# Attention ahead of two MLPs on one core: K transposed like Q, small products in row tiles, bounds by TensorE, and a new order of steps

## The chip, the core and the metric

The kernel runs on one core of a Trainium2 chip. The metric is the device time of one launch in microseconds (us), taken as the median of three runs. A profile of one further execution goes with it. TensorE's matrix products are called PE here, its weight loads PEld, VectorE DVE, ScalarE ACT, GpSimd POOL, and the queue that issues the DMAs SP.

## The reference, cut to what matters

Three parts follow one another. Attention works on two batches of eight heads, 576 positions of 64 numbers, everything in float32:

```python
# factor 4: q, k, v are averaged over groups of 4 positions -> 144 positions
out_d = softmax(q_d @ k_d.T / 8) @ v_d            # whole attention over 144
out_up = repeat(out_d, 4)
mask = abs(pos_q - pos_k) < 4                     # local attention, 7 keys wide
out_local = softmax(where(mask, q @ k.T / 8, -1e9)) @ v
x = out_up + out_local                            # 1152 tokens x 512
```

Then a soft mixture of eight experts, `out += P[:, e] * (relu(x @ w1[e]) @ w2[e])` with `P` from eight rounds of row and column normalisation of a gate, and an MLP with a Mish activation and widths 512, 2048, 512.

## The kernel before, in words

Big products run in float16: each operand is split into a high and a low float16 part after it was scaled by a power of two, and three products replace one. The scale comes from a bound of the operand, so the kernel needs a bound of V (for x), of W1[0], of W2[0], of W1[1] and of the gate before it can split them.

Work is laid out by pairs of heads: pair j of batch b holds two heads in 128 partitions. Pairs 0 to 3 are batch 0, pairs 4 to 7 batch 1. One string, `ORDER`, lists the steps of the eight pairs and of the first expert; the program emits them in that order, and each engine takes its instructions strictly as they were emitted. A step may name its engine (`:V` DVE, `:A` ACT, `:G` POOL). The steps, with the pair's number behind the name:

- LQ, LK, LV, LW load q, k, v by groups of four (tile `vm`) and v by windows of 32 keys (tile `vw`).
- TP transposes 288 columns of q or k by PE (line 654); TQ (659) copies q's to `qt`, TK (558 or 556) k's to `kt`. `kt` holds the two heads of a pair in separate column blocks with zeros in the other head's partitions, so that one product over 128 partitions gives both heads. K is loaded in runs of six positions, so TK writes with a stride and in quarters. SQ and SK (677 on DVE, 681 and 682 on POOL) sum groups of four.
- Local scores: QL (690, 695) adds the mask and 24 products of 32 queries by 64 columns. LM, SU, EL, LS, LN (711 to 737) are the softmax, TR (744) transposes 32 by 32 blocks on DVE, BD (558, 556) copies four pieces of it to a block-diagonal tile `bd`, AV (811) multiplies by `vw`.
- Averaged attention: QD (704), DM (759), ED (770), DS (776), DN (783), AP (794) transposes, AE copies, AD (819) multiplies by `vd`, which VP (627, 628) sums from `vm`.
- UP (825), XF (831), XH (837), XL (840) join both, scale them, and write the two float16 parts of x.
- VQ (619) squares `vm`, WM (175) squares or takes the maximum of a quarter of a weight tensor, WT, WP, WR, WQ, WE turn the partial bounds into a scale; WH and WL (195, 226) write the two parts of W1[0] and W2[0].
- M and R (914, 923) are the products of the first expert's first layer for one block of 128 features and 288 tokens; here tokens of batch 0 only. H and I write its float16 parts, N and E (1069) are the second layer for 128 tokens.

M needs x of all four pairs of batch 0, because it sums over all heads, and both parts of W1[0]. From the first M on, the steps of batch 1 stand between M and N. After `ORDER` come the gate (1137), the products of batch 1, seven more experts and the last MLP; nothing in them is touched. PSUM has eight banks: two for M and N, six for attention (`at`), of which QD and AV take two each.

Of the kernel before, what the change touches and what calls it, by code (L numbers as in the profile page):

```python
# [10 lines left out]
F32 = mybir.dt.float32  # L11
# [10 lines left out]
def attn_moe_moe2_kernel(ctx: ExitStack, tc: tile.TileContext, q, k, v, w_gate, w1, w2, w_in, w_out, out):  # L22
# [124 lines left out]
    class Split:  # L147
# [35 lines left out]
        def bound(self):  # L183
            m1 = sm.tile([128, 1], F32, tag="m1", name="m1")
            nc.vector.tensor_reduce(out=m1, in_=self.mx, axis=AX.X, op=ALU.add if self.squares else ALU.max)
            return m1

# [312 lines left out]
    ones = const.tile([128, 128], F32, name="ones")  # L500
    ss = const.tile([128, B, NP], F32, name="ss")
# [10 lines left out]
    spare_at, spare_dve = acc[:, NTT - 5, 0:384], acc[:, NTT - 4, :]  # L512
    spare_pool = acc[:, NTT - 3:NTT - 1, :].rearrange("p t d -> p (t d)")
# [7 lines left out]
    def emit_consts(t, mask):  # L521
# [13 lines left out]
        nc.vector.tensor_copy(out=ident16, in_=ident)  # L535
        nc.vector.memset(ones, 1.0)
        nc.vector.memset(ss, 0.0)
# [4 lines left out]
        nc.vector.tensor_copy(out=mask.rearrange("p g h c -> p (g h) c"),  # L542
                              in_=edge.unsqueeze(1).to_broadcast([128, 2 * G, 32]))

        nc.vector.memset(mask[0:32, 0, :, 0:3], SHUT)
        nc.vector.memset(mask[96:128, G - 1, :, 27:32], SHUT)
# [5 lines left out]
    spare_up = []  # L552

    def copy_on(eng, out, in_):
        if eng == "A":
            nc.scalar.activation(out=out, in_=in_, func=AF.Copy)  # L556
        else:
            tensor_engine(eng).tensor_copy(out=out, in_=in_)

    xs = [None, None]  # L560

    class Attention:
        def __init__(self, b, pools, at_tile):
            self.b, self.p, self.at = b, pools, at_tile
            self.qm, self.km, self.vm, self.vw, self.st = {}, {}, {}, {}, {}

        def load_qk(self, src, j):

            t = self.p["qk"].tile([96, 12, D], F32, tag="qk", name="qk")
            for h in range(2):  # L570
                a = src[self.b, 2 * j + h]
                if src is q:
                    nc.sync.dma_start(out=t.rearrange("p (u h) d -> p u h d", h=2)[:, :, h],
                                      in_=a.rearrange("(u p) d -> p u d", p=96))
                else:
                    nc.sync.dma_start(out=t[:, 6 * h:6 * h + 6], in_=a.rearrange("(p u) d -> p u d", u=6))
            return t

        def load_vm(self, j):

            t = self.p["vm"].tile([HM, 2, 2, 4, D], F32, tag="vm", name="vm")
            nc.sync.dma_start(out=t.rearrange("p h a r d -> p (h a) (r d)"),
                              in_=v[self.b, 2 * j:2 * j + 2].rearrange("h (a p r) d -> p (h a) (r d)", a=2, r=4))
            self.vm[j] = t
# [32 lines left out]
        def VQ(self, j):  # L617
            t = self.vm[j]
            nc.scalar.activation(out=spare_act[0:HM, :], in_=t.rearrange("p h a r d -> p (h a r d)"), func=AF.Square,
                                 accum_out=ss[0:HM, self.b, j:j + 1])  # L620

        def VP(self, j, eng):
            t = self.vm[j]
            vd = self.p["vd"].tile([HM, 2, 2, D], F32, tag="vd", name="vd")
            eng, room = (nc.vector, spare_dve) if eng == "V" else (nc.gpsimd, spare_pool)
            v2 = room[0:HM, 0:512].rearrange("p (h a r d) -> p h a r d", h=2, a=2, r=2)
            eng.tensor_tensor(out=v2, in0=t[:, :, :, 0:2, :], in1=t[:, :, :, 2:4, :], op=ALU.add)
            eng.tensor_tensor(out=vd, in0=v2[:, :, :, 0, :], in1=v2[:, :, :, 1, :], op=ALU.add)
            self.st["vd", j] = vd

        def bound(self):
            m1 = sm.tile([128, 1], F32, tag="mv", name="mv")
            nc.vector.tensor_reduce(out=m1, in_=ss[:, self.b, :], axis=AX.X, op=ALU.add)
            return m1

        def scale(self, ma):
# [3 lines left out]
            self.sxq = const.tile([128, 1], F32, name=f"sxq{b}")  # L640
            nc.vector.tensor_scalar(out=self.sxq, in0=self.sx, scalar1=0.25, scalar2=None, op0=ALU.mult)
# [7 lines left out]
        def TP(self, j, n, i):  # L649

            t = self.st["qk"[n], j]
            ps = self.at()[:, 0:288]
# [5 lines left out]
        def TQ(self, j, i):  # L658
            nc.scalar.activation(out=keep["qt"][j % 2][:, 288 * i:288 * i + 288], in_=self.st["T", j, 0, i],
                                 func=AF.Copy, scale=QSC)  # L660

        def TK(self, j, h, u, eng):

            to = keep["kt"][j % 2][64 * h:64 * h + 64, h, 3:3 + S].rearrange("c (p u r) -> c u p r", u=3, r=2)
            copy_on(eng, to[:, :, :, u],
                    self.st["T", j, 1, h][64 * u:64 * u + 64].rearrange("c (u p) -> c u p", u=3))

        def SQ(self, j, eng):
            self.pool_sum(keep["qd"][j % 2].unsqueeze(1), keep["qt"][j % 2][:, 0:S].unsqueeze(1), eng)

        def SK(self, j, eng):
            self.pool_sum(keep["kd"][j % 2], keep["kt"][j % 2][:, :, 3:3 + S], eng)

        def pool_sum(self, out, t, eng):
            t = t.rearrange("c h (m r) -> c h m r", r=4)
# [3 lines left out]
            n = out.shape[1]  # L679
# [1007 lines left out]
```

## Time and profile before

| | |
|---|---|
| three runs | 998.66, 994.86, 996.56 us; median 996.56 |
| profiled execution, its own time | 997.51 us |
| its span, first to last instruction | 995.7 us, so 1.8 us lie around it |
| busy | PE 964.9 us (97%), DVE 678.6 (68%), ACT 533.6 (54%), POOL 74.9 (8%) |
| HBM | 73.15 MB read, 14.94 MB written, 88 GB/s over the span |
| TensorE's clock, mean | 0.985 of 2.4 GHz |

A busy PE is one with a product under way; the ends of products are modelled. The clock is given as a share: 1.00 is 2.4 GHz, 0.50 is 1.2 GHz, and what lies between is a mean over a stretch that had both.

### The profile page before, as it was taken

Reading aid. Unit: us, or ns where it says so; the run is one execution under the profiler, and the core shown is the slowest. Engines: PE = TensorE matmul, PEld = TensorE weight load, DVE = VectorE, ACT = ScalarE, POOL = GpSimd, SP = SyncE. Lnnn points to the kernel's source line nnn. Section 1 sums busy time; section 2 is a strip of 40 time slices with the busy share of each in tenths; the row PEclk is TensorE's granted clock in tenths of the full one; section 3 lists DMA queues with packets and bytes.
Section 4 is the critical chain, followed back from the end, with each engine's and each line's share of the span. In section 5 each row is a group of like instructions: output and inputs, shape, how many; then the busy total and the mean of one; then the engine's idle time right before and its main releaser. Section 6 shows DMA issues by size and latency. Waiting matters only on the chain. (4 is left out here: it accounts for less than half of the span.)

```text
span 995.7 us, 17815 instructions
## 1 busy us (share of the span) xinstructions
PE 964.9 (97%) x7201; PEld 654.5 (66%) x7201; DVE 678.6 (68%) x1361; ACT 533.6 (54%) x1019; POOL 74.9 (8%) x122
## 2 busy tenths in 40 slices
PE   6889998999999999999999999999999999999998
PEld 4666574675477457547745764674476667888897
DVE  8878667687858947794895679387757356545531
ACT  6658545477367638636672864477284132433331
POOL 5671300000000000000000000000000000000000
PEclk8689999999999999999999999999999999999999
DMA  9861220212413152222424232331303702000010
GB/s 209 175 173 53 62 86 1 85 65 64 152 60 117 53 170 75 95 97 95 133 80 148 85 98 70 130 127 56 114 2 120 303 2 85 12 12 18 7 64 32
DMA packets 75917, 89.23 MB, mean 90 GB/s; under 512 B 25404, under 2 KB 60220, under 8 KB 74556
## 3 DMA queue, kind: packets, MB, share of 16 engines
q1 hardware_dynamic: 75836, 88.11, 28.2%
q8 instruction: 56, 0.92, 0.4%
q14 instruction: 25, 0.20, 0.1%
HBM read 73.15 MB, written 14.94 MB: 88 GB/s over the span
## 5 line engine op out<-in xcount | busy, mean ns | idle before, releaser
L1069 PE MATMUL mm<-wbh,h 128*128 128x512 f16 x1152 | 353.2, 379 | 2.6 <-ACT h L556 2.4
L1069 PEld LDWEIGHTS <-h 128*128 128x128 f16 x1728 | 168.5, 98 | 194.3 <-ACT h L556 2.9
L1069 PE MATMUL mm<-wbl,h 128*128 128x512 f16 x576 | 218.3, 379 | 0.0
L1038 PE MATMUL mm<-x,wah 128*128 128x288 f16 x672 | 128.1, 286 | 0.0
L1004 DVE SCALAR_TENSOR_TENSOR r<-mm,s 128x288 f32<-128x288 f32 x168 | 75.0, 454 | 71.3 <-PE mm L1038 64.3
L1038 PEld LDWEIGHTS <-wx 128*128 128x128 f16 x1008 | 98.6, 98 | 30.7 <-issue 6.0
L1469 PE MATMUL mm<-xc,win 128*128 128x256 f16 (+1 forms) x960 | 107.6, 262 | 0.0
L1000 ACT ACTIVATE s<-mm 128x288 f32<-128x288 f32 x168 | 66.4, 413 | 74.6 <-PE mm L1038 74.3
L1038 PEld LDWEIGHTS <-wah 128*128 128x128 f16 x896 | 87.7, 98 | 26.5 <-issue 0.6
L1038 PE MATMUL mm<-xt,wx 128*128 128x288 f16 x672 | 97.0, 286 | 4.1 <-DVE r L1004 4.0
L1038 PE MATMUL mm<-x,wal 128*128 128x288 f16 x336 | 96.1, 286 | 0.0
L1469 PEld LDWEIGHTS <-win 128*128 128x128 f16 x960 | 87.2, 98 | 13.3
L1478 ACT ACTIVATE tt<-mm,cf 128x512 f32<-128x512 f32 (+1 forms) x40 | 25.8, 645 | 113.1 <-PE mm L1469 111.3
L1013 DVE SCALAR_TENSOR_TENSOR h<-r,h 128x576 f16<-128x576 f32 x112 | 81.4, 749 | 0.6 <-ACT h L1012 0.6
L1012 ACT ACTIVATE h<-r 128x576 f16<-128x576 f32 x112 | 74.4, 680 | 11.2 <-DVE r L1004 10.9
L1485 DVE TENSOR_TENSOR tt<-tt 128x128 f32<-128x128 f32 x128 | 31.6, 288 | 69.4 <-ACT tt L1478 68.3
L1102 DVE SCALAR_TENSOR_TENSOR acc<-mm,pc,acc 128x512 f32<-128x512 f32 x63 | 47.0, 746 | 32.2 <-PE mm L1069 32.0
L98 POOL PARTITION_ALL_REDUCE ma<-m x25 | 11.4, 457 | 663.0 <-DVE m L241 379.2
L237 ACT ACTIVATE junk<-raw 128x1024 bf16<-128x1024 f32 x52 | 54.9, 1056 | 0.3
L1038 PEld LDWEIGHTS <-wal 128*128 128x128 f16 x448 | 43.8, 98 | 11.0
L411 ACT ACTIVATE junk<-w 128x512 bf16<-128x512 f32 x32 | 20.1, 630 | 57.2 <-DVE w L404 41.4
L1038 PE MATMUL mm<-x,wx 128*128 128x288 f16 x336 | 50.3, 286 | 0.0
(245 smaller groups left out, 1433.3 us busy)
## 6 DMA issues: line engine op xcount, KB each, us to landing
raw<-in_moe_w_dram SPq DMA_DIRECT2D x32, 1024.0 KB, 5.1
f<-in_moe_w_in_dram SPq DMA_DIRECT2D x16, 512.0 KB, 4.3
f<-in_moe_w_out_dram SPq DMA_DIRECT2D x16, 512.0 KB, 5.9
scr<-st SPq DMA_DIRECT2D x32, 256.0 KB, 2.3
scri<-st SPq DMA_DIRECT2D x16, 256.0 KB, 2.5
win<-scri SPq DMA_DIRECT2D x2, 2048.0 KB
vw<-in_v_dram SPq DMA_DIRECT2D x30, 96.0 KB, 2.7
qk<-in_k_dram SPq DMA_DIRECT2D x16, 144.0 KB, 4.3
```

Of the source, the lines that this page charges most:

```text
L237: nc.scalar.activation(out=junk, in_=r[:, c * 1024:(c + 1) * 1024], func=AF.Square, accum_out=mx[:, 2 * i + c:2 * i + c + 1])
L411: nc.scalar.activation(out=b, in_=w, func=AF.Square, accum_out=mq[:, f // 8:f // 8 + 1])
L1000: nc.scalar.activation(out=t, in_=ps, func=AF.Copy, scale=HSC)
L1004: nc.vector.scalar_tensor_tensor(out=out, in0=ps, scalar=HSC, in1=r, op0=ALU.mult, op1=ALU.add)
L1012: lows.append((n + 3, lambda: nc.scalar.activation(out=hi, in_=r, func=AF.Relu)))
L1013: lows.append((n + 6, lambda: nc.vector.scalar_tensor_tensor(out=lo, in0=r, scalar=0.0, in1=hi, op0=ALU.max, op1=ALU.subtract)))
L1038: nc.tensor.matmul(ps, lhsT=w.part(wi, a)[:, c:c + 128], rhs=factor(b, bn, xi, i), start=(not before and k == 0), stop=(k == 5), skip_grou ...
L1069: nc.tensor.matmul(ps, lhsT=h[ft][:, hi, t * 128:(t + 1) * 128], rhs=wt[:, ws], start=(ft == 0 and n == 0), stop=(ft == FT - 1 and n == 2))
L1102: nc.vector.scalar_tensor_tensor(out=a, in0=ps, scalar=pc[:, t:t + 1], in1=a, op0=ALU.mult, op1=ALU.add)
L1469: nc.tensor.matmul(ps[:, q_ * n:(q_ + 1) * n], lhsT=win[q_][:, wi, f, ws], rhs=x[:, xi, kk, :], start=(m == 0), stop=(m == 3 * KT - 1))
L1478: nc.scalar.activation(out=tt[:, 0:2 * n], in_=ps, func=AF.Mish, scale=coef[c][:, f:f + 1])
L1485: nc.vector.tensor_tensor(out=a[o], in0=a[u], in1=a[v], op=op)
```

## The change

K is loaded and transposed exactly as Q is, and `kt` holds 128 partitions by 576 without zeros. QL, QD and AV multiply 64 partitions at a time: head 0 uses the upper 64 rows of the array and head 1 the lower 64, each into a PSUM bank of its own. AV multiplies blocks of 64 keys (48 columns each); BD becomes one multiplication by a 0/1 tile `half`. For batch 0 the sums of V by four come from PE (VP with `pool_w`, then the copy VE); for batch 1 the old sums stay (now named VS). The bound of V for batch 0 and of W1[0] comes from products of the tensors' high halves with themselves (VG, WG), of which DVE takes the greatest entry (VR, WD); for batch 1 ACT squares `vw`. The scale of x moves from UP and XF to XH and XL, and XL always runs on DVE. FL issues products of a constant tile: none for `:A`, one for `:V`, two for `:G`. Attention's PSUM becomes two single banks (`at`) and two tiles of two banks (`att`). `ORDER` is written anew.

```diff
         def bound(self):
...
+        def squares_of(self, i, at):
...
+            self.gram[i] = at()
+            products_of(self.gram[i], self.parts[i])
+
+        def greatest(self, i):
+            nc.vector.tensor_reduce(out=self.mx[:, i:i + 1], in_=self.gram[i][:, 0:128], axis=AX.X, op=ALU.max)
...
+    def products_of(ps, t):
+
+        high = t.bitcast(BF16).rearrange("p (n c w) -> p n c w", c=128, w=2)[:, :, :, 1]
+        n = high.shape[1]
+        for i in range(n):
+            nc.tensor.matmul(ps[:, 0:128], lhsT=high[:, i], rhs=high[:, i], start=(i == 0), stop=(i == n - 1))
...
+        def VP(self, j):
+            ps = self.at()
+            for g in range(G):
+                i, k = g % 3, g // 3
+                nc.tensor.matmul(ps[32 * i:32 * i + 32, 128 * k:128 * k + 128], lhsT=pool_w, rhs=self.vw[j][:, :, g, :],
+                                 start=True, stop=True, tile_position=(0, 32 * i))
...
-        def TK(self, j, h, u, eng):
-
-            to = keep["kt"][j % 2][64 * h:64 * h + 64, h, 3:3 + S].rearrange("c (p u r) -> c u p r", u=3, r=2)
-            copy_on(eng, to[:, :, :, u],
-                    self.st["T", j, 1, h][64 * u:64 * u + 64].rearrange("c (u p) -> c u p", u=3))
+        def TQ(self, j, i, eng):
+            copy_on(eng, keep["qt"][j % 2][:, 288 * i:288 + 288 * i], self.st.pop(("T", j, 0, i))[:, 0:288], QSC)
+
+        def TK(self, j, i, eng):
+            copy_on(eng, keep["kt"][j % 2][:, 3 + 288 * i:291 + 288 * i], self.st.pop(("T", j, 1, i))[:, 0:288])
...
-                nc.tensor.matmul(sl[32 * jj:32 * jj + 32, 64 * g:64 * g + 64], lhsT=qt[:, 24 * n:24 * n + 32],
-                                 rhs=kt[:, :, 24 * n:24 * n + 32], start=False, stop=(n >= 20),
-                                 tile_position=(0, 32 * jj))
+                for h in range(2):
+                    p = slice(64 * h, 64 * h + 64)
+                    nc.tensor.matmul(sl[32 * jj:32 * jj + 32, h, 32 * g:32 * g + 32], lhsT=qt[p, 24 * n:24 * n + 32],
+                                     rhs=kt[p, 24 * n:24 * n + 32], start=False, stop=(n >= 20),
+                                     tile_position=(64 * h, 32 * jj))
...
-                nc.tensor.matmul(sd[a][0:HM, 0:2 * SD], lhsT=qd[:, a * HM:(a + 1) * HM],
-                                 rhs=kd.rearrange("c h m -> c (h m)"), start=True, stop=True)
+                for h in range(2):
+                    p = slice(64 * h, 64 * h + 64)
+                    nc.tensor.matmul(sd[0:HM, h, a * SD:(a + 1) * SD], lhsT=qd[p, a * HM:(a + 1) * HM], rhs=kd[p, :],
+                                     start=True, stop=True, tile_position=(64 * h, 0))
...
+        def AV(self, j):
+            vw, bd = self.vw[j], self.st.pop(("bd", j))
+            self.st["vv", j] = vv = self.at2()
+            for g in range(G):
+                for r in range(2):
+                    p = slice(64 * r, 64 * r + 64)
+                    for par in range(2):
+                        nc.tensor.matmul(vv[64 * par:64 * par + 64, r, 48 * g:48 * g + 48], lhsT=vw[p, par, g, :],
+                                         rhs=bd[p, G * par + g].rearrange("p e q -> p (e q)"), start=True, stop=True,
+                                         tile_position=(64 * r, 64 * par))
...
+        def XL(self, j):
+            nc.vector.scalar_tensor_tensor(out=xs[self.b][:, 1, j, :], in0=self.st.pop(("xf", j)), scalar=self.sx,
+                                           in1=xs[self.b][:, 0, j, :], op0=ALU.mult, op1=ALU.subtract)
...
-        "LK0 LK1 TP0.1.0 LQ0 TP0.1.1 TK0.1.0:A TK0.0.0:A TP1.1.1 TK0.1.1:V TP1.1.0 TP0.0.1 LQ1 LV1 TK1.1.1:A "
+        "LK0 TP0.1.0 LQ0 FL5:V LK1 TP0.1.1 TP0.0.1 LK2 TP0.0.0 TK0.1:A TK0.0:A FL23:G LQ1 LD0.1 TQ0.1:A LQ2 TQ0.0:V "
...
-        mm_banks(2)
-        at_p = ps_pool("at", 6, att_cm)
+        mm_banks(1)
+        mm_banks(1)
+        at_p, at2_p = ps_pool("at", 2, att_cm), ps_pool("att", 2, att_cm)
```

Two places show how instructions move. The first is PE's queue just ahead of the first M. Before, it reads as follows (`ident` is the identity, used for transposes and to add the mask; a number behind x counts equal rows):

```order
L695 MATMUL at<-kt_140,qt_138 32x64 x8
L106 MATMUL at<-ident,m_701 1x128
L690 LDWEIGHTS ident_82
L690 MATMUL at<-mask,ident_82 128x384
L695 MATMUL at<-kt_141,qt_139 32x64 x16
L113 MATMUL at<-mrow,ones 128x1
L695 MATMUL at<-kt_141,qt_139 32x64 x8
L695 MATMUL at<-kt_140,qt_138 32x64 x8
L654 MATMUL at<-ident,qk 128x96 x9
L695 MATMUL at<-kt_140,qt_138 32x64 x8
L914 LDWEIGHTS wah
L914 MATMUL mm_972<-x,wah 128x288
```

In the changed kernel the last rows of PE's queue up to the first M are these:

```order
L753 MATMUL att<-kd_150,qd_148 72x144 x4
L704 MATMUL at<-ident,qk 128x96 x6
L736 LDWEIGHTS ident_82
L736 MATMUL att<-mask,ident_82 128x192
L736 LDWEIGHTS ident_82
L736 MATMUL att<-mask,ident_82 128x192
L743 MATMUL att<-kt_147,qt_145 32x32 x32
L704 MATMUL at<-ident,qk 128x96 x3
L743 MATMUL att<-kt_147,qt_145 32x32 x16
L106 MATMUL at<-ident,m_1118 1x128
L969 LDWEIGHTS wah
L969 MATMUL mm_1302<-x,wah 128x288
```

QL has 48 products of 32 columns in place of 24 of 64, with two mask products of 192 columns in place of one of 384. QD has four products of 144 columns in place of two of 288, and one QD of batch 1 (the first row) has moved ahead of the first M. The products that give the scale of W2[0] (`mrow`) no longer stand there.

The second place is DVE's queue in the early part of attention. Before, from the eleventh step after the constants on (`kt` and `kd` are K transposed and K summed by four, `qd` the same of Q):

```order
L558 COPY kt_140<-at 64x3x96 x2
L677 TENSOR_REDUCE kd_144<-kt_140 128x288
L558 COPY kt_141<-at 64x3x96
L677 TENSOR_REDUCE qd_142<-qt_138 128x144
L677 TENSOR_REDUCE kd_145<-kt_141 128x288
L759 TENSOR_REDUCE dnm<-at 72x2 x2
L677 TENSOR_REDUCE qd_143<-qt_139 128x144
L711 TENSOR_REDUCE lmx<-at 128x12
L716 TENSOR_TENSOR sl<-at,lmx 128x384
```

In the changed kernel DVE's queue reads at the same place:

```order
L591 TENSOR_SCALAR qt_144<-at 128x288
L723 TENSOR_REDUCE kd_150<-kt_146 128x144
L759 TENSOR_REDUCE lmx<-att 128x12
L764 TENSOR_TENSOR sl<-att,lmx 128x384
L803 TENSOR_REDUCE dnm<-att 72x4
L591 TENSOR_SCALAR qt_145<-aty 128x288
L775 TENSOR_REDUCE lsu<-sl 128x12
```

The strided copies to `kt` are gone from DVE (ACT makes all copies to `kt`), one sum by four is left, of half the size, and a copy of Q has come to DVE for some pairs.

## Rows read from the trace of the kernel before

**Rows 1.** By stage: length, busy PE, PEld, DVE, ACT, POOL (instructions), clock, DMA share, GB/s.

```profile
0.00:63.65 63.65, 44.61 (x561) 33.19 (x561) 51.16 (x117) 40.60 (x97) 43.98 (x70) 0.76 0.82 184
63.65:127.65 64.00, 63.65 (x592) 41.97 (x587) 48.85 (x108) 43.95 (x109) 18.81 (x26) 1.00 0.30 78
127.65:995.70 868.05, 856.69 (x6055) 579.31 (x6055) 578.60 (x1138) 449.06 (x816) 12.13 (x27) 1.00 0.25 84
```

**Rows 2.** Timeline of PE, first 80 us: start, length, line, tile, shape, count.

```profile
3.87 2.45 PE L654 MATMUL at<-ident,qk 96*128 96x96 f32 x12 [3.87 <-DVE ident L534]
...
14.09 0.88 PE L695 MATMUL at<-kt,qt 128*32 128x64 f32 x48
...
62.39 0.96 PE L654 MATMUL at<-ident,qk 96*128 96x96 f32 x9
...
63.65 0.42 PE L914 MATMUL mm<-x,wah 128*128 128x288 f16 x2
```

**Rows 3.** Groups on DVE, 0 to 63.65 us: count, busy us, mean ns.

```profile
L558 DVE COPY kt<-at 64x288 f32<-64x288 f32 x15 | 10.1, 673 | 0.5 <-ACT kt L556 0.2
...
L776 DVE TENSOR_SCALAR ds<-dsu 72x4 f32<-72x4 f32 x4 | 4.6, 1162 | 0.0
...
L677 DVE TENSOR_REDUCE qd<-qt 128x144 f32<-128x576 f32 x4 | 2.9, 722 | 0.0
L677 DVE TENSOR_REDUCE kd<-kt 128x288 f32<-128x1152 f32 x2 | 2.7, 1344 | 0.1
...
L558 DVE COPY atd<-at 72x288 f32<-72x288 f32 x5 | 2.1, 436 | 0.0
...
L110 DVE TENSOR_REDUCE mrow<-at 1x1 f32<-1x128 f32 x3 | 0.8, 258 | 5.3 <-PE at L106 5.3
...
L840 DVE TENSOR_TENSOR x<-xf,x 128x576 f16<-128x576 f32 x1 | 0.7, 737 | 0.0
```

**Rows 4.** Groups on POOL, 0 to 63.65 us.

```profile
L558 POOL COPY bd<-acc 32x288 f32<-32x288 f32 x12 | 9.0, 748 | 6.1 <-PE at L811 4.2 <-DVE acc L744 1.5
L627 POOL TENSOR_TENSOR acc<-vm 72x512 f32<-72x512 f32 x7 | 8.9, 1266 | 1.1 <-DMA vm<-in_v_dram 1.0
```

**Rows 5.** Timeline of PE, 99.8 us and later, at the full clock.

```profile
99.89 1.21 PE L811 MATMUL at<-bd,vw 128*64 128x96 f32 x24
101.03 0.43 PE L695 MATMUL at<-kt,qt 128*32 128x64 f32 x16
101.39 0.44 PE L794 MATMUL at<-ident,ad 72*72 72x72 f32 x4
101.67 0.38 PE L1069 MATMUL mm<-wbh,h 128*128 128x512 f16 x1
...
102.78 0.72 PE L819 MATMUL at<-atd,vd 72*64 72x144 f32 x8
103.43 0.39 PE L1069 MATMUL mm<-wbh,h 128*128 128x512 f16 x1
```

**Rows 6.** The same timeline, two later places.

```profile
106.68 1.13 PE L704 MATMUL at<-kd,qd 128*72 128x288 f32 x4
107.65 0.38 PE L1069 MATMUL mm<-wbh,h 128*128 128x512 f16 x1
...
127.65 2.35 PE L1137 MATMUL lp<-wg_hl,x 128*128 128x16 f16 x80 [0.26 <-DVE mc L76]
129.86 0.41 PE L914 MATMUL mm<-x,wah 128*128 128x288 f16 x2
```

**Rows 7.** Busy time in two stretches of attention (columns of rows 1).

```profile
18.70:36.00 17.30, 12.36 (x129) 8.57 (x129) 15.09 (x38) 11.91 (x30) 11.33 (x16) 0.52 1.07 216
...
43.50:60.00 16.50, 10.53 (x99) 9.33 (x100) 11.81 (x22) 10.13 (x16) 12.81 (x13) 0.60 0.56 157
```

**Rows 8.** DMA, 10 to 12 us: packets, bytes, sizes.

```profile
DMA packets 1427, 0.34 MB, mean 168 GB/s; under 512 B 1402, under 2 KB 1427, under 8 KB 1427
```

**Rows 9.** Timeline of DVE: XF of batch 1's first pair.

```profile
105.35 0.94 DVE L831 SCALAR_TENSOR_TENSOR xf<-at,sx,h 128x288 f32<-128x288 f32 x2
```

More of the change, by code (lines that the diff above doesn't have):

```diff
@@ L500, in attn_moe_moe2_kernel @@
     ones = const.tile([128, 128], F32, name="ones")
+    pool_w = const.tile([128, 32], F32, name="pool_w")
+    half = const.tile([128, 2], F32, name="half")
     ss = const.tile([128, B, NP], F32, name="ss")
@@ new lines, in emit_consts @@
+        nc.vector.memset(mask[96:128, G - 1, 27:32], SHUT)
+        near = t[:, 5, 0:8]
+        nc.vector.scalar_tensor_tensor(out=near, in0=col[:, 0:8], scalar=-4.0, in1=row[:, 0:8], op0=ALU.mult,
+                                       op1=ALU.add)
+        nc.vector.tensor_scalar(out=near, in0=near, scalar1=-4.5, scalar2=None, op0=ALU.add)
+        nc.vector.tensor_tensor(out=near, in0=near, in1=near, op=ALU.mult)
+        for i in range(4):
+            p = slice(32 * i, 32 * i + 32)
+            nc.vector.tensor_scalar(out=pool_w[p, 6 * i:6 * i + 6], in0=near[p, 0:6], scalar1=4.0, scalar2=None,
+                                    op0=ALU.is_lt)
@@ L617, in VQ @@
         def VQ(self, j):
[L618 to L626, printed above, removed]
+            t = self.vw[j].rearrange("p h g d -> p (h g d)")
@@ L651, in TP @@
             t = self.st["qk"[n], j]
[L652 removed]
+            ps = at_y() if self.b == 0 and i else self.at()
             for u in range(3):
@@ L754, in DM, with ad @@
[L754 to L761 removed]
+        def ad(self, j):
+            t = keep["ad"][j % 2]
+            if self.rows:
+                return t[:, :, :, :, 0:24]
+            return t.rearrange("p h a g c -> p (h a g c)")[:, 0:4 * SD].rearrange("p (h a g c) -> p h a g c", h=2, a=2, g=G)
@@ L828, in XF @@
[L828 to L834 removed]
+            n = 96 if self.rows else HM
@@ new lines, in filler, with at2_tile @@
+        def filler(i, eng):
+            ps = mm_pools[0][0].tile([128, 512], F32, tag=mm_pools[0][1], name="fill")
+            for _ in range("AVG".index(eng)):
+                nc.tensor.matmul(ps, lhsT=warm[:, 0:128], rhs=warm, start=True, stop=True)
+        def at2_tile():
+            return at2_p.tile([128, 2, 512], F32, tag="att", name="att")
+        keep = {n: [pools["keep"].tile(sh, F32, name=f"{n}{i}") for i in range(2)]
+                for n, sh in (("qt", [128, S + 8]), ("kt", [128, S + 8]), ("qd", [128, SD]), ("kd", [128, SD]),
+                              ("ad", [HM, 2, 2, G, 32]))}
@@ L1204, in attn_moe_moe2_kernel @@
+        nc.gpsimd.memset(warm, 1.0)
+        nc.gpsimd.memset(half, 0.0)
+        for i in range(4):
+            nc.gpsimd.memset(half[32 * i:32 * i + 32, i % 2:i % 2 + 1], 1.0)
+        nc.gpsimd.memset(ones, 1.0)
+        nc.gpsimd.memset(ss, 0.0)
+        nc.gpsimd.memset(pool_w, 0.0)
         for i in range(2):
-            nc.gpsimd.memset(keep["kt"][i][0:64, 1], 0.0)
-            nc.gpsimd.memset(keep["kt"][i][64:128, 0], 0.0)
-            nc.gpsimd.memset(keep["kt"][i][:, :, 0:3], 0.0)
@@ L1216, in attn_moe_moe2_kernel @@
-        A = [Attention(b, pools, at_tile) for b in range(B)]
+            nc.gpsimd.memset(keep["ad"][i].rearrange("p h a g c -> p (h a g) c")[:, :, 24:32], 0.0)
+        A = [Attention(b, pools, at_tile, at2_tile) for b in range(B)]
         A[0].new_vw(0)
         nc.gpsimd.memset(A[0].vw[0][0:32, 0, 0, :], 0.0)
+        emit_fields()
+        lib = pools["keep"].tile([128, 16], F32, name="lib")
+        nc.gpsimd.memset(lib, 0.0)
+        nc.gpsimd.tensor_tensor(out=lib[:, 0:8], in0=lib[:, 0:8], in1=lib[:, 8:16], op=ALU.add)
```

258 lines of the change are left out of this document (126 added, 132 removed), and 53 rows, old and new, of the table ORDER.

## The prediction

> **What bounds the kernel now.** I read the busy time by stage first. The kernel falls into three stages, cut where PE starts the first M (63.65 us) and where the gate starts (127.65 us). In the last two stages PE is busy 63.65 of 64.00 us and 856.69 of 868.05 us at clock 1.00; in the first it is busy 44.61 of 63.65 us at a mean clock of 0.76 [rows 1]. So the reader is to see two different things. From the first M on, PE's own work sets the time, and an instruction saved on DVE, ACT or POOL is worth nothing. Before the first M, PE waits, and the time is set by how fast all engines together bring x of batch 0 and W1[0] to the two float16 parts. There DVE is the fullest, 51.16 us of 63.65, or 80%; POOL has 43.98, ACT 40.60 [rows 1].
>
> Next the timelines of PE, which give the moment of the first M, and what a step costs PE from its first product to the first product of the next step [rows 2, 5, 6]. Last the groups on DVE and POOL in the first stage, for what there is to take away [rows 3, 4].
>
> The sum therefore has three terms: how much earlier the first M starts, how much PE work the second stage has, and which new waits stand in it. The third stage is taken as it is; its instructions don't change. I work on the profiled execution, 997.51 us (995.7 us of span and 1.8 us around it), which is 0.95 us above the median of the three runs. The runs span 994.86 to 998.66 us, so about 0.5% is what can be told from no change.
>
> **First stage, DVE.** Removed: 15 strided copies to `kt`, 10.1 us; four sums of q by four, 2.9; two sums of k of double width, 2.7; five copies of transposed weights (`atd`, now on ACT), 2.1 [rows 3]. That is 17.8 us. Added: one sum of k of half the width, 0.7; four copies of q at the price of `atd`, 436 ns, 1.7; three more XL at 737 ns, 2.2; one multiplication of the averaged weights (DN of pair 1), by the same row 0.7; six maxima over 128 columns of PSUM (VR, WD) by the reduction at 258 ns, 1.5 [rows 3]. LM and SU of one more pair are two passes over 384 numbers, between 436 and 722 ns each [rows 3], 1.2 together; the constants for `pool_w` I put at 1.0. That is 9.0 us, and DVE comes to 51.2 - 17.8 + 9.0 = 42.4 us.
>
> One more item is a wait inside an instruction. DS adds a constant to 72x4 numbers and takes 1162 ns on average, against 737 ns for a 128x576 pass [rows 3]: it is held up while POOL works. Four of these cost 4.6 us. POOL loses its 12 copies to `bd` (9.0 us) and its seven large sums of V (8.9 us, and their second halves) [rows 4], and gets four multiplications of 576 columns and more small sums; I count it at about half of its 44 us. So between 0 and 4.6 us of DVE's time comes back; I take half, 2.5 us. DVE then has 39.9 us. At the present 80% this gives a first M at 49.6 us.
>
> **First stage, PE.** It gains work, and has to be counted too. Prices at the full clock:
>
> QL took 0.88 us for 48 records (a float32 product is two), 18 ns each [rows 2]. The new one has 96 records of half the columns. If all eight positions of the array overlap as the four do now, it takes 0.44 us; if a record costs what it costs now, 1.76 us; and at the smallest spacing that a product with a full weight load shows, 80 in 2.21 us or 27.6 ns [rows 6], 2.65 us. I take 1.76, since at 18 ns a record of 64 columns already comes close to what four positions allow, and 32 columns gain little. QD took 0.97 us [rows 6]; between 0.49 (both halves of the rows at once) and 0.97, I take 0.7. AV took 1.14 us for 24 records, 47.5 ns each [rows 5]; now 48 records of half the columns, between 0.57 and 2.28 us, I take 1.0. AD took 0.65 us [rows 5]; with two column positions in turn 0.33 to 0.65, I take 0.4. AP stays at 0.28 us for four [rows 5], TP at about 0.32 for three (0.96 for nine) [rows 2]. The 56 bfloat16 products of VG and WG have no row: from 27.6 ns [rows 6] to 47.5 ns [rows 5] each, 1.5 to 2.7 us, I take 2.7. VP has 48 records, at 47.5 ns 2.3 us. The seven filler products have the shape of N's, 0.38 us at most [rows 5], less when they follow each other: 2.
>
> Up to the first M the new queue holds QL of six pairs, 10.6 us; QD of five, 3.5; AV and AD of four, 4.0 and 1.6; VG, WG, VP and fillers, 7.0; 28 TP, 9.0; eight AP, 2.2. That is 37.9 us; the old one at the same prices has 27.2. So PE gets nearly as full as DVE. PE starts at 3.87 us, when the identity is ready [rows 2], so it could not reach M before 41.8 us. With two engines that full and each waiting for the other, I put the first M at 50 us, 13.65 us earlier. From below it is bounded by PE without a wait, 42 us, of which I use 44; from above by the clock, under the rivals.
>
> The TensorEngine Tiling (Array Packing) page of the Trainium skill, section Instruction Overhead, speaks against this part: a product has an overhead of some 60 cycles, so that one column takes as long as sixty, and a small dimension should not be cut for tiling. QL cuts 64 columns to 32. At 2.4 GHz 60 cycles are 25 ns, an estimate from that page, and QL would take 2.4 us a pair, AV 1.2; the trace's 18 ns for records of 64 columns lies below it, so four positions do overlap here, and what eight do no row shows.
>
> **What hides the rest.** K now lands in packets of 256 bytes like Q. In two microseconds of such packets the queues moved 0.34 MB, 168 GB/s [rows 8]. Q and K of four pairs are 2.4 MB and V 1.6 MB, 24 us at that rate, and W1[0]'s 2.1 MB come to 12 us even so: 36 us, well ahead of 50, and V is no longer loaded twice for batch 0. ACT loses its copies for `bd`, its squares of V and W1[0], and stays behind DVE. These I cost at nothing; if the first M came by 40 us, the loads would be the next to bind.
>
> **Second stage.** PE is full there, so the difference of its work counts in full. Removed and added: QD four at 0.97 to three at 0.7, -1.8; QL of two pairs, +1.8; AV of four, -0.6; AD of four, -1.0; one TP less, -0.3. Together -1.9, say -2 us. The ends of the prices give -7.2 and +6.8 us. For new waits I add 1 us: today PE idles 0.35 us there [rows 1], and the tiles `att` and `at` are fewer than the six banks were.
>
> **Sum.** 997.51 - 13.65 - 2 + 1 = 982.9 us; less 0.95 for the median, 982 us. With the first M between 45 and 55 us and the second stage between -4 and +3 us its own range is 975 to 989 us.
>
> **Rivals.**
>
> Every record costs at least 27.6 ns. For it speaks the only row of such products [rows 6]; against it QL's 18 ns. QL then costs 0.89 us more a pair and AV 0.3. PE has 44.5 us in the first stage; used at 90% after 3.87 us, that is a first M at 53.3 us, a gain of 10.35. The second stage has 3.1 us more. 997.51 - 10.35 - 2 + 3.1 + 1 - 0.95 = 988 us. The rule of the Trainium skill above is this mechanism with 25 ns.
>
> The clock stays low. In attention the granted clock was 0.52 from 18.7 to 36 us and 0.60 from 43.5 to 60, while PE stood still for a quarter to a third of those stretches [rows 7]. If it keeps its mean of 0.76, the 37.9 us become 49.9; with PE used at 85% the first M is at 62.5 us. The gain is 1.1 us, and 997.51 - 1.1 - 2 + 1 - 0.95 = 994 us: no change. Against it: VG, WG and the fillers lie in these stretches, and a queue 10 us fuller leaves shorter gaps.
>
> The two `att` tiles hold up PE in the second stage, and the kernel is slower. QL, QD and AV take one each, nine times after the first M, and the next but one waits until it is read. The fourth pair's AV started at 99.89 us and its tile was read out by XF at 106.29 us, 6.4 us later [rows 5, 9]; M and N stand behind a waiting product on PE. The gain of 14.65 us is gone at 1.6 us a turn. At 2.4 us, 21.6 in all, it is 997.51 - 13.65 - 2 + 21.6 - 0.95 = 1002.5 us. Against it: between the turns stand runs of M and N of several microseconds.
>
> Nothing waits and all positions overlap: first M at 44 us, second stage -7.2: 997.51 - 19.65 - 7.2 - 0.95 = 970 us.
>
> **How the numbers follow.** Chances: the forecast 0.60, the 27.6 ns 0.13, the clock 0.14, the tiles 0.08, the best case 0.05. Faster by over 0.5% (below 991.6 us) are the first, the second, the last and a third of the clock's, 0.82; slower the tiles, 0.08; the rest, 0.10, is within 0.5%. The range of 974 to 995 us leaves out the best case and the tiles, and some of the tails.
>
> **What would show it.** The first M near 50 us; DVE with about 40 us of work before it and DS near 0.2 to 0.6 us; a run of 96 QL records in about 1.8 us; the clock at 1.00 for most of the first 50 us; the second stage, from first M to gate, near 63 us with PE idle for under 2 us. The prediction is wrong if the clock falls for more than 20 us, if the first M waits for a load, or if PE waits for `att` again and again.

## The result and the profile after

The changed kernel takes 984.24 us (median of four runs, 983.66 to 987.67) against 995.71 us of the kernel before measured beside it (994.39 to 998.66): ratio 0.9888, 95% interval [0.9855, 0.9921]. Timed again in another session it took 986.52 us (six runs, 985.02 to 990.54) against 997.9, ratio 0.9893 [0.9871, 0.9915]. The profiled execution took 987.67 us, the slowest of the first four and 3.4 us above their median, so the sums below show less than the median gained.

By stage, cut at the same two places as [rows 1] (columns as there):

```profile
0.00:52.55 52.55, 41.73 (x1083) 32.93 (x1087) 38.86 (x102) 31.68 (x88) 25.86 (x63) 0.94 0.87 197
52.55:117.00 64.45, 62.15 (x788) 40.86 (x786) 47.24 (x93) 36.56 (x98) 22.17 (x24) 0.97 0.32 82
```

The first M starts at 52.55 us in place of 63.65, 11.1 us earlier. In the second stage PE is busy for 1.5 us less than before, 62.15 for 63.65, yet the stage is 0.45 us longer. The third is 868.9 us for 868.05. Between the two profiled executions, 997.51 and 987.67 us, the sum -11.1 + 0.45 + 0.85 gives the whole difference.

What the second stage loses is one hole. The waits of PE before the first M, then after it (us in total, times, longest):

```profile
PE at L704 <- DVE mask_t L556: 4.2, 1, 4.2
PE att L743 <- issue: 2.7, 2, 2.2
PE att L753 <- POOL qd L727: 1.7, 1, 1.7
PE aty L704 <- ACT kt L587: 0.5, 1, 0.5
...
PE mm L969 <- issue: 2.3, 1, 2.3
```

The first line is the start, as in [rows 2]. No wait is for the tile `att` to come free, and none for a load. "issue" is time in which PE waited for no semaphore that the profile shows. The timeline of PE at these two places:

```profile
23.40 0.69 PE L743 MATMUL att<-kt,qt 64*32 64x32 f32 x43 [2.18 <-issue]
...
52.55 0.41 PE L969 MATMUL mm<-x,wah 128*128 128x288 f16 x2
...
57.10 0.28 PE L969 MATMUL mm<-x,wal 128*128 128x288 f16 x1 [2.30 <-issue]
57.22 0.41 PE L969 MATMUL mm<-x,wah 128*128 128x288 f16 x2
57.46 0.30 PE L969 MATMUL mm<-x,wal 128*128 128x288 f16 x1
57.58 0.66 PE L969 MATMUL mm<-x,wah 128*128 128x288 f16 x2
```

PE stops in the middle of a run of equal products, and behind the second hole the same product goes from 0.41 to 0.66 us, the lower clock. A second execution (e1 below) had the holes at the same records, 2.01 and 2.00 us long, and in its first stage the clock did not fall:

```profile
0.00:51.46 51.46, 41.40 (x1083) 32.48 (x1087) 38.34 (x102) 31.31 (x88) 25.86 (x63) 1.00 0.92 201
```

The clock column of such a row has a gap that matters here: it counts the time ahead of the clock's first rise as 1.00, and the products there say otherwise. In the same execution:

```profile
12.32 1.24 PE L753 MATMUL att<-kd,qd 64*72 64x144 f32 x8 [1.22 <-POOL qd L727]
...
14.94 0.69 PE L704 MATMUL at<-ident,qk 96*128 96x96 f32 x3 [0.22 <-issue]
...
16.23 0.47 PE L704 MATMUL aty<-ident,qk 96*128 96x96 f32 x3
...
18.33 0.71 PE L753 MATMUL att<-kd,qd 64*72 64x144 f32 x8
```

The same QD takes 1.24 us and later 0.71, three transposes 0.69 and later 0.47; in e9, at a granted 0.50, a QD takes 1.24 us as well (at 27.88 us). So PE ran at the lower level until the trace's first record of the clock: at 16.1 us here, 9.8 in the first profile, 12.7 in the kernel before (there twelve transposes took 2.45 us at 3.87 and nine 0.96 at 62.39 [rows 2]). With these starts at 0.50 the first stages come to 0.84, 0.84 and 0.66 in place of 1.00, 0.94 and 0.76, an estimate from these times. The clocks given below are the column's.

The groups on DVE before the first M that answer to [rows 3]:

```profile
L889 DVE TENSOR_TENSOR xf<-att,up 128x576 f32<-128x576 f32 x4 | 3.0, 745 | 0.2 <-ACT up L587 0.2
L591 DVE TENSOR_SCALAR qt<-at 128x288 f32<-128x288 f32 x3 | 1.4, 450 | 1.0 <-PE at L704 1.0
L820 DVE TENSOR_SCALAR ds<-dsu 72x4 f32<-72x4 f32 x4 | 1.1, 274 | 0.0
L723 DVE TENSOR_REDUCE kd<-kt 128x144 f32<-128x576 f32 x1 | 0.8, 754 | 0.0
```

No copy to `kt` is left on DVE, and DS is down from 1162 to 274 ns with POOL busy 25.86 us in place of 43.98. But other small instructions of DVE got longer: the copy `invx` went from 159 to 1133 ns, the scale `sx` from 221 to 784, four steps of `ident` from 188 to 401 each, together 2.4 us of the 3.5 that DS gave back.

### The profile page after: what moved, and what is told of

It is laid out like the page before. It is cut to its first block, busy times and chain, and to the rows that moved or that the text cites. A ratio compares the mean times of both kernels' runs of the same rounds, so it can differ in the third digit from the quotient of the medians.

```text
span 985.9 us, 19187 instructions
## 1 busy us (share of the span) xinstructions
PE 962.0 (98%) x7925; PEld 653.4 (66%) x7928; DVE 665.2 (67%) x1333; ACT 517.6 (53%) x1000; POOL 60.2 (6%) x114
## 3 DMA queue, kind: packets, MB, share of 16 engines
q1 hardware_dynamic: 82316, 86.93, 27.6%
## 5 line engine op out<-in xcount | busy, mean ns | idle before, releaser
L98 POOL PARTITION_ALL_REDUCE ma<-m x25 | 11.4, 458 | 669.5 <-DVE m L258 385.8
L1093 PEld LDWEIGHTS <-wal 128*128 128x128 f16 x448 | 43.8, 98 | 11.1
L428 ACT ACTIVATE junk<-w 128x512 bf16<-128x512 f32 x32 | 20.1, 629 | 57.2 <-DVE w L421 41.4
```

Source lines behind the costliest of these rows:

```text
L1093: nc.tensor.matmul(ps, lhsT=w.part(wi, a)[:, c:c + 128], rhs=factor(b, bn, xi, i), start=(not before and k == 0), stop=(k == 5), skip_grou ...
```

## Experiments

The theory at this point: the gain is the earlier first M; it comes from work taken off DVE, ACT and POOL. The rivals: PE's clock, which fell before and now does not, is the gain itself; or PE's own work alone sets the first M. Each experiment is told with its first M and the mean clock of its first stage; the changed kernel had 52.55 us at 0.94, and 51.46 us at 1.00 in its second profile.

**e1, the changed kernel again.** No edit.

> The changed kernel as it is, timed again, to narrow the ratio and to see which of its two standstills of PE recur. PE stood still from 21.2 to 23.40 us inside QL of pair 2 and from 54.8 to 57.10 us inside the first M, with no semaphore to wait for, each time while one packet of 16 KB of the instruction queue was under way. Theory (PE's next instructions come late behind full data queues): both holes stand at the same instruction, lengths between 1 and 3 us, median 984 us within 1.5. Rival (a chance event of that one execution): other places or none, and the median of runs without them nearer to 981.

986.52 us, 1 us past the expected range. The holes stand at the same records (x43 left in QL, the same `wal` product in M), 2.01 and 2.00 us. The place is not chance.

```profile
23.81 0.58 PE L743 MATMUL att<-kt,qt 64*32 64x32 f32 x43 [2.01 <-issue]
...
55.70 0.28 PE L969 MATMUL mm<-x,wal 128*128 128x288 f16 x1 [2.00 <-issue]
```

**e2, K in runs again.**

```diff
-in_=src[self.b, 2 * j + h].rearrange("(u p) d -> p u d", p=96)        (k as q)
+in_=a.rearrange("(p u) d -> p u d", u=6)                               (k alone)
-copy_on(eng, keep["kt"][j % 2][:, 3 + 288 * i:291 + 288 * i], ps[:, 0:288])
+to = keep["kt"][j % 2][64 * i:64 * i + 64, 3:3 + S].rearrange("c (p u r) -> c u p r", u=3, r=2)
+for r in range(2): copy_on(eng, to[:, :, :, r], ps[64 * r:64 * r + 64, 0:288].rearrange("c (u p) -> c u p", u=3))
```

> Undoes one part: K is loaded in runs of six rows again, and each of its two transposed blocks is copied to kt by two strided copies of 64 partitions (675 ns each in the kernel before) in place of one of 128 (406 ns). Theory (the gain of the change is the earlier first M, and it comes from work taken off the other engines): ACT, which has the 15 copies of K in the first stage, gets 15 x 0.94 = 14 us more and is as full as DVE was; first M at 57 to 62 us in place of 52.55, time 988 to 994 us. Rival (PE's own work alone sets the first M now): 984 us within 2. Rival on the standstills (packets of 256 bytes make them): with K in packets of 1536 bytes both holes shrink below 1 us, which would take up to 3 us off either time.

992.97 us, ratio 0.9943 [0.9921, 0.9965]; first M at 62.93. The stage, one of the groups of `kt` on ACT, and the stretch from 44 us to the first M:

```profile
0.00:62.93 62.93, 51.13 (x1084) 39.17 (x1088) 39.20 (x105) 45.91 (x104) 25.57 (x64) 0.82 0.79 181
```
```profile
L587 ACT ACTIVATE kt<-at 64x288 f32<-64x288 f32 x20 | 13.7, 683 | 0.9 <-PE at L708 0.4
```
```profile
44.00:62.93 18.93, 17.74 (x345) 13.40 (x345) 11.23 (x22) 12.97 (x27) 2.62 (x4) 0.50 0.55 139
```

ACT did get 14 us more, and the time is the theory's (the first M a microsecond past its range). But from 44 us to the first M it is PE that is full, 17.74 of 18.93 us, at the lower clock, and ACT is not: there PE's own work sets the end, as the rival has it, though not at the rival's time. The holes shrank to 0.64 us in QL and to none in M, as the third theory had it; but they do so in e5 and e6 too, where the packets are left as they were, so the size of the packets is not shown to be the reason. It gained nothing here.

**e3, bounds on ACT again.**

```diff
-products_of(ps, self.vw[j].rearrange("p h g d -> p (h g d)"))          (VG; VR and WD now empty)
+self.VQ(j)
-WG=lambda i, n: max_of(i).squares_of(n, at_tile)
+WG=lambda i, n: [max_of(i).measure(2 * n + k, "A") for k in range(2)]
```

> Undoes one part: the bounds of V and W1[0] are sums of squares on ACT again (four squares of V at about 1.0 us, four of W1[0] at about 1.25 us, 9 us on ACT) in place of 56 products on PE (some 3.6 us) and six maxima on DVE (1.65 us). Theory (PE, DVE and ACT each near 80% and waiting for each other): ACT goes from 31.7 to 41 us of 52.6, PE and DVE get less; the two nearly cancel, first M between 51 and 56 us, time 982 to 988 us. Rival (these products matter because they keep PE's clock up): mean clock of the first stage from 0.94 to below 0.88, first M after 56 us, time above 988 us.

991.16 us, ratio 0.9933 [0.9912, 0.9955]; first M at 57.70, clock 0.89. The stage, and ten microseconds behind the hole in QL:

```profile
0.00:57.70 57.70, 40.52 (x1028) 30.64 (x1031) 38.83 (x99) 39.37 (x107) 27.39 (x65) 0.89 0.90 188
```
```profile
24.00:34.00 10.00, 8.49 (x147) 6.54 (x147) 5.25 (x16) 7.68 (x26) 2.13 (x3) 0.52 0.86 160
```

The hole before this stretch was 3.71 us long, and the clock lay at its lower level behind it. First M and time are the rival's, the clock just misses its mark of 0.88. PE had less work than in the changed kernel and came later. But the rival's mechanism is not shown by it: PE stood without a wait for 6.6 us in QL, 2.7 us in the changed kernel, and this run can't tell the missing products from the longer holes.

**e4 and e8, sums of V on POOL again.**

```diff
-ROWS = (0,)    ... LW2 VP0 SK2:G VE0:A ...          VP1 ... VE1:A ...
+ROWS = ()      LV0 ... SK1:G VS0:G ... LW1 LV1 ...   VS1:G LV2 ...
```

> Undoes one part: V of batch 0 is loaded a second time (4 x 288 KB) and its sums of four rows are made by POOL (two additions, about 2.0 us a pair) in place of 12 products with pool_w on PE and a copy on ACT; the transposed averaged weights have 72 rows again. Theory (DVE instructions are held up while POOL works, so POOL's work comes back on DVE): POOL from 25.9 to 33 us in the first stage, additions of constants to small tiles on DVE (251 ns now) back above 500 ns, DVE 1 to 3 us fuller, first M 0 to 3 us later, time 983 to 988 us. Rival (PE alone sets the first M): four VP of 0.57 us less, first M 2 us earlier, 982 us.

996.84 us, ratio 0.9995 [0.9978, 1.0012]; first M at 65.05, clock 0.80. The theory's price was far too low: this one part undone takes the whole gain. POOL came to 36.4 us and DVE to 43.5, 4.6 us more than in the changed kernel, with DS at 435 ns, under the 500 expected. The timeline of POOL shows the first reason:

```profile
19.20 1.26 POOL L666 TENSOR_TENSOR acc<-vm 72x512 f32<-72x512 f32 x1 [5.77 <-DMA vm<-in_v_dram]
20.54 0.72 POOL L667 TENSOR_TENSOR vd<-acc 72x256 f32<-72x256 f32 x1
21.22 0.66 POOL L726 TENSOR_TENSOR acc<-qt 128x288 f32<-128x288 f32 x1
```

POOL stands 5.77 us for the load, and the averages of q for QD are queued behind it; PE then waits 5.1 us for `qd`.

> The undo of the sums of V by PE once more, for a second look at the run in which POOL stood 5.8 us for the load of V of pair 0 with the averages of q queued behind it. Same kernel, so the same wait within 2 us, the same fall of the clock after it (0.50 to 0.67 from 20 to 32 us) and a first M within 2 us of 65.

996.1 us in one run, first M at 65.38, clock 0.50 to 0.72 from 20 to 32 us: repeated, with the clock a little above the range expected.

**e9, the same with POOL's sum of pair 0 later.**

```diff
-SK1:G VS0:G ... LW1 LV1 ... LW2 SK2:G DM1
+SK1:G       ... LW1     ... LW2 SK2:G VS0:G LV1 DM1
```

> The sums of V on POOL again, but with POOL's sum of pair 0 behind the averages of q and k of pairs 1 and 2 (where the changed kernel copies VP of pair 0), so that its load has landed by then; loads of the later pairs follow it. Theory (the earlier undo lost its time because POOL stood 5.8 us for a load with the averages queued behind it, and PE's clock fell in the gap): PE waits for qd under 1.5 us each, clock above 0.92 to the first M, first M at 53 to 57 us, 985 to 989 us. Rival (the 8 us of work on POOL are themselves what costs): first M after 60 us, 993 us or more.

996.84 us, ratio 0.9990 [0.9970, 1.0011]; first M at 65.75. The theory fell: without the stand for `qd` the time is the same. First M and time are the rival's, but the longest wait in the profile is for a load and not for POOL. The long waits of PE, two rows of the queue that issues the loads, and the stretches from 24 us:

```profile
PE at L583 <- DMA raw<-in_moe_w_dram: 4.2, 1, 4.2
PE att L753 <- POOL qd L727: 1.7, 1, 1.7
```
```profile
16.38 0.31 SPq L657 DMA_DIRECT2D vm<-in_v_dram  x1
16.73 0.40 SPq L158 DMA_DIRECT2D raw<-in_moe_w_dram  x1
```
```profile
24.00:36.00 12.00, 9.93 (x167) 8.30 (x168) 7.26 (x19) 5.38 (x14) 5.40 (x7) 0.50 0.95 167
36.00:50.00 14.00, 13.69 (x230) 10.38 (x211) 10.04 (x21) 6.91 (x21) 13.09 (x15) 0.50 1.15 184
50.00:65.75 15.75, 14.34 (x284) 11.18 (x284) 12.47 (x21) 8.79 (x19) 6.00 (x7) 0.52 0.77 175
```

PE waits 4.2 us once, for the second load of W1[0]. It is issued right behind one more load of V, 0.29 MB (the other three follow it), and 1.6 us later than in the changed kernel, 16.73 us for 15.13. In that gap the clock falls, and it stays at the lower level for the 40 us to the first M, while PE is busy 37.96 of 41.75 us. Whether the loads alone would do it, or POOL's 8 us with them, was not taken apart.

**e5, no fillers.**

```diff
 def filler(i, eng):
+    return
```

> The changed kernel without its seven filler products (they take 0.2 us each at the full clock; nothing reads them). Theory (PE's clock in the first stage hangs on PE's gaps being short): gaps grow, the mean clock of the first stage falls from 0.94 to 1.00 to 0.85 to 0.95, first M at 52 to 57 us, time 985 to 991 us. Rival (fillers are only work): first M 1.5 us earlier, 983 to 985 us. On the standstills of PE without a wait: if they come from the fetch of PE's instructions, they move with the count of instructions, to 4 products later in QL of pair 2 (39 records behind the hole in place of 43) and 7 products later in M; if from the place in the program, they stay where they are.

984.44 us, ratio 0.9877 [0.9838, 0.9916]; first M at 51.61, clock 1.00. In this execution the fillers keep up nothing that falls without them; of the four timed runs one has a mean clock of 0.989 and took 991.33 us, the others 0.998 to 0.999. The timeline shows the hole of QL:

```profile
22.53 0.33 PE L743 MATMUL att<-kt,qt 64*32 64x32 f32 x25
23.60 0.54 PE L743 MATMUL att<-kt,qt 64*32 64x32 f32 x39 [0.74 <-issue]
```

Four filler products less ahead of it, and the hole stands exactly four records later in the program, with 39 left for 43: it goes by the count of PE's instructions, as the theory of the fetch has it. In M no hole was left, and the one in QL was 0.74 us in place of 2.0 to 2.2 although the loads are the same; the theory had neither.

**e6, QL's heads one after the other.**

```diff
-for n in range(8 * part, 8 * part + 8): ... for h in range(2):
+for h in range(2): for n in range(8 * part, 8 * part + 8): ...
```

> QL issues all records of head 0 and then all of head 1 (same records, same sums) in place of the two heads in turn, so that neighbouring records lie on the same half of the rows. Theory (a record costs 12 ns because the two halves of the rows work side by side): 96 records take about 1.76 us in place of 1.15, six pairs 3.7 us more before the first M and 1.2 after it; first M 1 to 4 us later, time 986 to 991 us. Rival (12 ns is the rate at which PE takes records whatever their place): 1.15 us again and 984 to 986.5 us.

985.54 us, ratio 0.9866 [0.9840, 0.9893]; 96 records take 1.23 us, from 8.93 to 10.16 us, for 1.15 in the changed kernel (8.60 to 9.75 us in its first profile):

```profile
8.93 1.30 PE L743 MATMUL att<-kt,qt 64*32 64x32 f32 x96
10.16 0.74 PE L704 MATMUL aty<-ident,qk 96*128 96x96 f32 x3
```

Both stand ahead of the clock's first rise. At the full clock the 96 records of pair 2 take 1.01 us here (0.32 and 0.69), and those of pair 5 took 1.00 us in e1 (0.72 and 0.28, each to the start of the next step):

```profile
49.95 0.76 PE L743 MATMUL att<-kt,qt 64*32 64x32 f32 x64
50.67 0.47 PE L704 MATMUL at<-ident,qk 96*128 96x96 f32 x3
51.07 0.35 PE L743 MATMUL att<-kt,qt 64*32 64x32 f32 x32
51.35 0.27 PE L106 MATMUL at<-ident,m 128*1 128x128 f32 x1
```

The rival holds: a turn between the two row halves is not what makes them cheap.

**e7, later loads.**

```diff
-EL1 LW1 LS1 ... LW2 VP0 ... QL2.2 AP0.1 ...  LD1.1 M5.0 LV4 R0.1 TK7.0:A LW7 ... VQ5 R5.0
+EL1     LS1 ...     VP0 ... QL2.2 LW1 LW2 AP0.1 ... M5.0 R0.1 TK7.0:A ... VQ5 LD1.1 LV4 LW7 R5.0
```

> Four loads are issued later: those of V of pairs 1 and 2 behind QL of pair 2 instead of ahead of it, and those of W2[0]'s second half and of V of pair 4 and 7 behind the first R of block 5, with the maximum that needs W2[0] after them. Theory (PE's next instructions come late because the data queues are full): the holes of 2.0 to 2.2 us in QL of pair 2 and of 2.0 to 2.3 us in M shrink below 1 us, 1 to 3 us gained, 982 to 985 us in place of 985 to 986.5. Rival (the fetch takes that long whatever the data queues hold): the holes keep 2 us, time 985 to 988 us.

984.81 us, ratio 0.9865 [0.9843, 0.9886]. The holes shrank, at the same record in QL and near it in M:

```profile
23.48 0.57 PE L743 MATMUL att<-kt,qt 64*32 64x32 f32 x43 [0.54 <-issue]
...
55.68 0.42 PE L969 MATMUL mm<-x,wah 128*128 128x288 f16 x2 [0.42 <-issue]
```

The second stage took 61.17 us, from 52.89 to 114.06. The holes came out as the theory has it, but that the loads did it is not shown: e5 and e6, with the loads where they were, also have short holes (0.74 us and none in QL, none and 1.73 us in M), and the data queue was no emptier around this one. From 20 to 24 us its packets took this share of the 16 engines, for 101.2% in the changed kernel:

```profile
q1 hardware_dynamic: 3169, 0.79, 118.5%
```

Of the time, the intervals of e1 and e7 overlap, so a gain is not shown.

**e10, more work on DVE.**

```diff
+def dve_more(): nc.vector.tensor_tensor(out=acc[:, 0, :], in0=acc[:, 1, :], in1=acc[:, 2, :], op=ALU.add)
+DX = dve_more, 16 times in ORDER between QD0 and M0.0
```

> The changed kernel with 16 additions of 128x512 numbers on DVE that nothing reads, spread evenly over its order before the first M; by the rows of 128x384 (0.55 us) and 128x576 (0.75 us) some 0.65 us each, 10.4 us in all, about what the copies to kt cost DVE before the change. Theory (the prediction's: DVE's work sets the first M, at about 80%): 10 to 13 us later, first M at 61 to 65 us, 994 to 998 us. Rival (PE's own 41 us set it and DVE has 13 us of slack): first M before 56 us, under 990 us. Between the two: both bind.

991.75 us, ratio 0.9948 [0.9928, 0.9968]; first M at 61.49.

```profile
0.00:61.49 61.49, 47.95 (x1086) 36.63 (x1087) 51.39 (x122) 32.70 (x91) 29.41 (x64) 0.84 0.81 180
```
```profile
L1266 DVE TENSOR_TENSOR acc<-acc 128x512 f32<-128x512 f32 x16 | 12.6, 786 | 0.0
```
```profile
46.00:61.49 15.49, 15.41 (x292) 11.53 (x272) 14.20 (x24) 8.55 (x20) 3.02 (x4) 0.50 0.59 139
```

These are the first stage, the group of the additions, and the last stretch before the first M. The additions cost 12.6 us, and the first M moved by 9 to 10 us in this execution. But it ends with 15 us at the lower clock in which PE is never idle. The ten runs tell the two apart: the three with the highest mean clock (0.995, 0.995, 0.997) took 988.93, 989.42 and 989.50 us, the one with the lowest (0.983) 995.69. So 12.6 us on DVE cost some 3 us over e1 where the clock held best, and up to 9 where it did not; at the median it is 5.2 us. Both bind: by these numbers the clock is the smaller part at the median and the larger one in the slowest runs. The edit is not DVE's alone either: POOL's sums of k (`acc` from `kt`) went from 742 to 1161 ns and POOL from 25.86 to 29.41 us.

**e11, the kernel before with fillers.**

```diff
+FL4 TP3.1.1, FL10 QL2.0, FL3 AP0.0, FL3 WP4, FL8 WR0, FL18 AV3.0   (FLn: n products of a constant 128x512 tile)
```

> The kernel before with 46 filler products (0.2 us each at the full clock, nothing reads them) on PE ahead of the six places where PE waits longest in its first stage, to keep its clock up and change nothing else. Rival (the change gains because PE's clock no longer falls): mean clock of the first stage from 0.76 to above 0.90, first M at 54 to 58 us, ratio to the kernel before below 0.995. Theory (the other engines' work sets the first M there, and the clock follows from PE's waits): the clock rises, first M moves by less than 2.5 us, ratio 0.997 to 1.002.

999.19 us, ratio 1.0014 [0.9993, 1.0035]; first M at 63.31.

```profile
0.00:63.31 63.31, 48.69 (x606) 32.33 (x606) 48.11 (x116) 40.81 (x97) 42.78 (x70) 0.95 0.87 185
```

The clock went from 0.76 to 0.95, the first M by 0.34 us. So in the kernel before a higher clock alone brings nothing that can be measured, and the clock alone is not the gain. That the other engines set the pace fits, as PE still idles 14.6 us; that the fillers' own work, some 9 us at 0.2 us each, took back part of a gain is not excluded.

**e12, later loads and no fillers.** The edits of e5 and e7 together.

> The changed kernel with the four later loads and without the fillers, a version that may beat both. Theory (each takes something of its own: shorter holes, 1.5 us less filler work): gate at 112 to 113.5 us, 982.0 to 984.0 us. Rival (holes and fillers only shift time among themselves): 984 to 986 us, as each alone.

985.76 us (983.74 to 993.86), ratio 0.9897 [0.9862, 0.9933]: the rival's. In the profiled run the holes were 0.21 and 0.78 us, but PE waited 2.8 us for `qd` and the clock still fell from 44 to 56 us. No version tried is shown to beat the changed kernel.

## Why the prediction was right, point by point

The forecast was 982 us; the time is 984.24, within its range, and the order of events is the one that it gave.

- **First M at 50 us.** 52.55 and 51.46 in two profiles, inside 45 to 55. Two of the 52.55 us are the hole in QL, which no step had.
- **DVE 39.9 us.** 38.86 us were measured, and DS came down to 274 ns, within 0.2 to 0.6. The share was 74%, not 80%. As a cause, the step is half right. e10 puts as much work back on DVE and loses about half of the gain (5.2 of 11.4 us), in part because the clock fell; where it held best, a microsecond on DVE cost about a quarter of one. At that price the 12.3 us that DVE lost are worth some 3 us, an estimate, of the 11.1 by which the first M moved. That a share of 80% gave the right time is in part luck.
- **PE's prices.** QL was mis-sized: 1.15 us for 96 records ahead of the clock's first rise, 12 ns each, and 1.00 us at the full clock, 10.4 ns, in place of 1.76; below the 18 ns taken and well below the 27.6 of the first rival. AV 0.84 (1.0 said) and VP 0.57 a pair (2.3 in all) fit. AD at 0.65 gained nothing from two column positions (0.4 said), and WG's 16 products took 1.01 us, 63 ns each, above the upper end of 47.5. The two mask products ahead of QL, 0.26 to 0.45 us a pair, were left out of the sum.
- **Loads hidden.** Yes: in two profiles no product waited for a load after the start. But with little to spare: in e9, with one more load of 0.29 MB ahead of it, PE waited 4.2 us for W1[0].
- **Second stage, -2 us of work and +1 of waits.** Without holes of 2 us it takes 61.36 us (e5) and 61.17 (e7), near -3. The wait was 2.0 to 2.3 us in the two profiles of the changed kernel, and a lower clock behind it, and not where the prediction looked: PE's own next instructions came late, not the tiles. The third stage, taken as it is, was 0.85 us longer in the first profile and 1.8 in the second.

The rivals: every record at 27.6 ns is refuted by QL (10.4 to 12 ns) and not by WG (63 ns). The section Instruction Overhead of the TensorEngine Tiling (Array Packing) page of the Trainium skill says that a small dimension costs as much as sixty columns; QL's 10.4 to 12 ns do not agree with it. The tiles `att` never held PE up. The clock is the rival that came nearest. The mean of 0.76 that it took from [rows 1] leaves out the slow start and was nearer 0.66 (the estimate above). In the changed kernel the column gives 0.94 to 1.00, but four edits that undo one part or add work (e2, e4, e9, e10) end in much what that rival described: first M at 61.5 to 65.8 us, mean clock 0.84 to 0.66, and in e2, e9 and e10 PE full at the lower level.

So the gain has one condition that the prediction gave only as a rival. With the clock up from its first rise on, PE is busy for 41.4 us and the first M comes at 51.46 (e1); in e9, at the lower level from 24 us on, PE is busy for 53.13 us and the first M comes at 65.75. What lets the clock fall is not one thing. At gaps of 2.1 to 5.1 us between 17 and 27 us it fell in the changed kernel's first profile, in e3, e4, e9 and e10, and not in e1 at one of 2.0 us. It came back within some 10 us, but for e9. In e2 and e10 it fell once more, at 43 and 45 us, with no wait of PE over 1.4 us in the ten before. The clock is the likely reason why the parts do not add up: over e1, undoing K costs 6.5 us, the bounds 4.6 and V's sums 10.3, together more than the whole gain of 11.4. What stays open: how much of V's price is the loads and how much POOL, and why the clock fell or came back in some executions and not in others of the same kernel. And no run takes back the new ORDER, the tiles of PSUM or the row tiles of QL, QD and AV by themselves, so what these are worth is not shown.

## What to carry to other kernels

When a change moves work from DVE and ACT to PE, look at whether PE would be the bound at its lower clock: if so, the change is worth its price only as long as the clock stays up, and an edit that looks free can cost the whole gain, as V's sums on POOL did here. A low clock in a profile is not in itself a loss; filler products raised it from 0.76 to 0.95 here and gained nothing. Compare the time of equal products too: here the clock of the first stage looked higher than it was, because its start was counted as full. Undo one part at a time, and read the clock of the stage with each time before putting a price on the part.

## What the runs showed of the hardware that was not expected

- PE can stop for up to 3.7 us with no semaphore to wait for, at places that go by the count of its instructions. Counted in all records of PE's queue (products, weight loads, semaphores), every such stop of 0.4 us or more stands behind 448, 704, 1216, 1728, 1982 or 2238 of them, within 1: apart by multiples of 256, within 2. This holds for all the profiles here; the kernel before, e9 and e11 have no such stop. The page of the changed kernel (busy us and records of PE and PEld; packets and MB of the queues) says what arrives there:

```profile
PE 962.0 (98%) x7925; PEld 653.4 (66%) x7928; DVE 665.2 (67%) x1333; ACT 517.6 (53%) x1000; POOL 60.2 (6%) x114
...
q8 instruction: 62, 1.02, 0.4%
```

  PE and PEld have 15853 records together and queue 8 has 62 packets, 256 records a packet; in the kernel before 14402 records and 56 packets, 257. So queue 8 brings PE's instructions, 16 KB at a time. The Runtime: NRT & Kernel Launch page of the Trainium skill, section Instruction fetch mechanics, states blocks of 256 instructions in 16 KiB, and that crossing from one to the next is mostly hidden. The traces agree with both: 62 packets go with three stops of 0.4 us or more in the changed kernel, 56 packets with none in the kernel before. From 20 to 24 us, around the hole in QL (share of 16 engines):

```profile
q1 hardware_dynamic: 2909, 0.73, 101.2%
q8 instruction: 1, 0.02, 2.0%
```

  The data queue fills all DMA engines while the one packet is under way, but that does not fix the length of the hole: it was 2.18 us at this share, 0.54 at 118.5% (e7), and in e6, with the same count and loads, there was none in QL of pair 2 and 1.73 us in M. What sets it stays open. The first stage has twice the PE records that it had before, 1083 and 1087 for 561 and 561 in less time, so it needs its blocks at least twice as often.
- Records of 64 rows by 32 columns follow each other at 12 ns ahead of the clock's first rise (12.8 ns when the row halves don't take turns), and at 10.4 and 10.5 ns at the full clock: the lower clock makes QD take 1.24 us for 0.71, but these little longer.
- PE begins at its lower level: the same products take about 1.8 times as long, from first product to next step, up to 9.8 us in one execution of the changed kernel and up to 16.1 in the other.
- Once at 0.50, the clock stayed there for some 40 us in e9 although PE was busy for 37.96 of 41.75 us.
